# Another order of the first eight steps, and eight weight sums moved from VectorE to TensorE

## The chip, the cores and the metric

The kernel runs on one core of one Trainium2 chip. The metric is the device time of one execution in microseconds; the time before is the median of three runs. Engines are named as in the profile: PE is the matmul engine TensorE (PEld its weight loads), DVE is VectorE, ACT is ScalarE, POOL is GpSimd, and SP is the engine on whose queue nearly all transfers are issued.

## What is computed

Linear attention without softmax, a normalisation by head, and a dense layer pair with softplus between its matrices:

```python
kv  = einsum('bhsd,bhse->bhde', k, v)          # 8 batches, 8 heads, 576 rows, 64 wide
out = einsum('bhsd,bhde->bhse', q, kv)
rms = sqrt(mean(out * out, -1) + 1e-6)
x   = (out / rms * g_norm) as 4608 x 512       # float32
h   = x @ w_in                                 # 512 x 2048, given in 64-bit floats
g   = softplus(h)
return g @ w_out                               # 2048 x 512, given in 64-bit floats
```

## The kernel before

**Tiles and stages.** The 4608 rows of x are 36 tiles of 128; three tiles make a block of 384 rows, twelve blocks in all. The 2048 hidden columns are sixteen chunks of 128. In the first stage blocks 0 to 3 are taken through chunks 0 to 3 and blocks 4 to 11 through chunks 0 to 5. One pair of block and chunk is a *step* (function `step`, 64 steps). `mm1` (L843) makes the chunk's h for the block in one PSUM bank of the ring `h`, ACT applies softplus (L865) and takes the high part (L867), DVE makes the low and the third part (L854, L858), and `mm2` (L850) adds the product with w_out to three sum banks `s0` to `s2`, one for each tile. When the block's chunks are done, `leave` evicts each sum bank with ACT (L895) and stores it to DRAM as a partial sum (L910). Two further phases, with blocks of 512 rows and pairs of chunks, take the rest by a scheme with seven products for eight (L1030, L1100). In the last phase `enter` loads a tile's two partial sums and adds them into the bank with which that phase begins (L886, L889), and `leave` writes the output.

**Precision.** Every matmul operand is cut into a high, a low and a third part in the format fp32r, and three matmuls stand for one product. `split` does it for x (L620, L623, L626), `split_weight` for the weights.

**Weights.** `weight(j, ...)` handles one of the 32 pieces, j = 2c for w_in of chunk c and j = 2c + 1 for w_out. It loads the 64-bit words (L403, 512 KB), and DVE and ACT turn them into one float: `square` (L414), `high1`, `high2`, `mask`, `power`, `rest` (L418, L422, L427, L435, L440) give a large part `t` and a small part `p`, and `total` (L444) adds the two on DVE into a buffer `w` of the SBUF ring `m`. `split_weight` then reads `w`: ACT takes the high part (L481 for w_in, L483 for w_out), DVE the low part (L488, L491), ACT scales the low part (L494). For chunks 0 to 3 (`by_pe`) PE forms the rest in an `h` bank (L505, L506), and ACT writes the third part from there (L509). The ring `h` has two banks.

**x.** `kv_of` forms kv of a batch on PE from K and V loads (L676). `rows(t)` makes one tile of x: q turned (L756, L763), product with kv (L700), square (L773), reduce (L704), root on POOL (L707, L708), norm (L712), turned by PE (L718) and, for tiles 0 to 5, split straight from the bank. x is also stored to DRAM (L782, L783); from tile 6 on, `x_again` loads and splits it. The split x of a block lies in one of two `xv` buffers, which the block gives back with the mm1 of its last chunk.

**What sets the order.** `Plan` writes out the order of every engine's queue beforehand. Each task has an engine, a price in ns, the tasks that it comes after, the buffers that it takes and gives, and a position `pos`. The planner takes, among the tasks that could begin within 150 ns of the first, the one with the smallest `pos`. A task's end, as its successors see it, is start + price + a hand-over of its engine (`HANDOVER`, 120 to 250 ns; L181, L194). Positions come from the number of the step and from lists of constants `P0` to `P7`: when each weight is fetched (`FETCH`) and converted (`CONVERT`), when rows are made, and so on. Where PE would stand idle early on, the planner puts in a filler, `warm` (L1181), a matmul of the identity whose result nobody reads; it ends with step 6.

The steps are listed by `ORDER` (L363), block by block. Besides its x and weights, the mm1 of step s waits for the mm1 before it and for the finished w_out of step s - 2 (L861, L862).

Of the kernel before, what the change touches and what calls it, by code (L numbers as in the profile page):

```python
# [8 lines left out]
F32 = mybir.dt.float32  # L9
# [4 lines left out]
ALU = mybir.AluOpType  # L14
# [4 lines left out]
P = 128  # L19
# [36 lines left out]
class Plan:  # L56
# [19 lines left out]
    def slot(self, ring):  # L76
        return Slot(ring)
# [11 lines left out]
    def order(self):  # L89
# [5 lines left out]
        ready = {}  # L95
# [28 lines left out]
        while left:  # L124
            best = None
            for engine, tasks in ready.items():
                options = []
                for t in tasks:
                    at = max(engine_free[engine], t.ready)
                    if t.size:  # L130
                        at = max(at, dma_free - 2500)
                    for i, s in enumerate(t.take):
                        others = sum(u.ring == s.ring for u in t.take[:i])
                        if engine == "SP" and s.ring in ("m", "n"):
                            others += self.KEEP
                        if len(free[s.ring]) <= others:
                            break
                        at = max(at, sorted(free[s.ring])[sum(u.ring == s.ring for u in t.take[:i])][0])
                    else:
                        options.append((at, t))  # L140
                if not options:
                    continue
                first = min(at for at, _ in options)
                options = [(at, t) for at, t in options if at <= first + self.SOON]
                small = [o for o in options if engine == "PE" and o[1].kind != "all"]
                if small:
                    rest = [o for o in options if o[1].kind == "all"]
                    if kind != "all":
                        options = [o for o in small if o[1].kind == kind] or small
                    elif rest and len(small) < self.TOGETHER and (  # L150
                            min(o[1].pos for o in small) + self.PATIENCE > min(o[1].pos for o in rest)):
                        options = rest
                at, t = min(options, key=lambda o: (o[1].pos, o[0]))
                if engine == "PE" and self.spare and self.spare[-1].start is None:
                    ring, run, ns, _ = self.spare
                    begin = max(engine_free["PE"], self.BEGIN, min(free[ring])[0] if free[ring] else at)
                    if begin + ns <= at:
                        s = Slot(ring)
                        at, t = begin, Task("PE", ns, lambda s=s: run(s), [], None, [s], [s], 0)
                        t.kind = "all"  # L160
                        s.readers = 1
                if best is None or at < best[0]:
                    best = (at, t)
            if best is None:
                raise RuntimeError("the plan is stuck at " + str([(e, t.pos, [s.ring for s in t.take if not free[s.ring]]) for e, ts in ready.items() for t in ts][:20]))
            at, t = best
            if t in ready[t.engine]:
                ready[t.engine].remove(t)
                left -= 1
            for s in t.take:  # L170
                place = min(free[s.ring])
                free[s.ring].remove(place)
                s.place = place[1]
                if t.pos is not None:
                    coming[s.ring] = coming.get(s.ring, 0) - 1
            if t.engine == "PE":
                t.ns += self.SWITCH.get((kind, t.kind), 0)
                kind = t.kind
            t.start = at
            engine_free[t.engine] = at + t.ns  # L180
            t.end = at + t.ns + self.HANDOVER[t.engine]  # L181
            if t.size:
                dma_free = max(dma_free, at + t.ns) + t.size
                t.end = dma_free + (self.LANDING if dma_free > self.FILLED else 2000)
            for s in t.give:
                s.readers -= 1
                last_read[id(s)] = max(last_read.get(id(s), 0), t.end)
                if not s.readers:
                    free[s.ring].append((last_read[id(s)], s.place))
                    retire(s.ring)  # L190
            for u in users.get(id(t), ()):
                waiting[id(u)] -= 1
                if not waiting[id(u)]:
                    u.ready = max([a.end for a in u.after] + ([u.follows.start] if u.follows else []), default=0)  # L194
                    ready.setdefault(u.engine, []).append(u)
            done.append(t)
        return sorted(done, key=lambda t: t.start)
# [3 lines left out]
def kernel(  # L201
# [24 lines left out]
    nc = tc.nc  # L226
    B, H, S, D = q.shape
    d_model, d_ff = moe_w_in.shape
# [17 lines left out]
    STEPS = [(ph, n, p) for ph in (1, 2) for n in range(n_wide) for p in PAIRS[ph - 1][n]]  # L246
    LAST = 2

    P0 = [-45.94, -26.77, -11.8, 0.28, -29.91, -5.64, -2.86, 3.84, -103.4, -98.98, -69.3, -76.66, -68.5, -24.67, -23.22, -34.97, 8.15, -43.02, 7.47, 9.69, 7.18, 18.16, -12.1, 4.75, 1.0, 95.98, -6.45, 6.38, 7.69, 5.17]
    P4 = [-30.17, -6.08, 16.93, -33.9, -22.35, -28.91, -17.33, -7.12, -9.75, -2.59, 0.87, 2.93, -12.14, -3.26, 0.98, 3.76, 7.8, -3.0, -2.25, 7.68, 20.89, 50.27, -0.5, -0.13, 26.66, 22.67, -11.61, -5.55, 2.74, 0.64, -0.48, 1.34, 0.64, 1.68, -8.4, -1.37]  # L250
    P5 = [1.24, -5.69, -2.28, 1.58, 5.58, 0.43, 5.83, -7.56, 3.01, -2.95, 3.18, 1.42, -14.52, 0.57, -1.29, -1.34]
    P6 = [-0.39, 4.6, -0.28, -2.24, -0.01, 1.05, 1.77, -3.9, -2.15, 0.85, 1.85, -1.74, 6.34, -2.44, -0.13, 3.82, 7.89, 0.51]
    P7 = [-23.78, -17.98, -11.85, -14.93, 0.41, 1.61, 7.35, 2.7, -25.02, -6.6, -15.2, -4.48, -2.14, 0.64, 2.93, 0.97, 4.67, 5.36, 3.33, 6.57, -10.37, 2.36, -14.11, -9.89, -7.11, 12.91, -2.89, 14.55, 12.59, 9.35]
    CONVERT, FETCH, EARLY, LATER = P0[:8], P0[8:16], P0[16:27], P0[27:]
    P1 = [48.8, 48.65, 66.31, 74.64, 125.35, 131.27, -11.31, 54.26, 67.75, 469.13, 282.82, 195.86]
    P2 = [22.14, 35.93, 25.02, 37.31, 52.38, 81.67, 74.61, 116.65, 106.27, 111.35, 100.82, -152.23, 99.52, 221.41, 428.54, -173.95, 119.58, -155.43, 317.87, 212.07, -7.69]
    P3 = [3.0, 2.86, 5.84, -16.31, 1.53, 3.03, 3.55, -20.64, 3.15, 2.55, 1.38, 1.52, 1.27, 0.75, 2.42, -1.39]
    SPLIT = {p: (P1[i], P1[6 + i]) for i, p in enumerate((2, 3, 4, 5, 6, 7))}
    TAKEN = {c: (P2[c - 6], P2[4 + c]) for c in range(6, 16)}
    LEAD, APART, AHEAD, MM2, LATE, SPLIT_G = P3[0], P3[1], P3[2], P3[3:11], P3[11:14], P3[14]  # L260
# [99 lines left out]
        return src[e * NP:(e + 1) * NP].rearrange("p s d -> s p d")  # L360


    ORDER = [(n, c) for n, cs in CHUNKS.items() for c in cs]  # L363
    first_step = {}
    last_step = {}
    for s, (n, c) in enumerate(ORDER):
# [27 lines left out]
    def weight(j, pos, fetch_pos, behind):  # L394

        c, of_out = divmod(j, 2)
        raw, w = slot("rawb" if j % 2 and c < 8 else "raw"), slot("m")
        words = 2 if wide else 1

        def fetch():  # L400
# [6 lines left out]
        if wide:  # L407
# [41 lines left out]
            d2 = add("DVE", 690, high2, [d1], pos, [], [raw])  # L449
            d3 = add("DVE", 690, mask, [d2, a1], pos, [])  # L450
            over_done.append(add("ACT", 910, beyond, [d3], pos + (4 if c < 4 else 0), [], [sq]))
            d4 = add("DVE", 430, power, [d3], pos, [p, w])
            d5 = add("DVE", 690, rest, [d4], pos, [], [raw])
            ready = add("DVE", 690, total, [d3, d5], pos, [], [t, p])
        else:
            ready = add("DVE", 450, lambda: nc.vector.tensor_copy(new(w, [P, d_model]), raw.tile[:, :, 0]),
                        [f], pos, [w], [raw])
# [370 lines left out]

    def step(s):
        n, c = ORDER[s]  # L830
        cs = CHUNKS[n]
        h, g, gv = slot("h"), slot("g"), slot("gv")
        if c == cs[0]:
            sums[:] = [slot(f"s{i}") for i in range(TB)]
# [21 lines left out]
        def less():  # L856
# [3 lines left out]

        a = add("PE", 2100, mm1, x_split[n] + factors_done[0, c] + [m for _, m in mm1s[-1:]] +  # L861
                (factors_done[1, ORDER[s - 2][1]] if s > 1 else []), s, [h],  # L862
                ([xv] if c == cs[-1] else []) + ([w_in] if s == last_step[c] and c != 4 else []))
        mm1s.append((s, a))
        a = add("ACT", 490, lambda: nc.scalar.activation(new(g, [P, NT]), h.tile, func=AF.Softplus, scale=1.0 + E),  # L865
                [a], s, [g], [h])
# [14 lines left out]
    def enter(t, bank, pos):  # L881

        both_of = []
        for src, st in part[t]:
            pt = slot("m")
            both_of.append((pt, add("SP", 350, lambda pt=pt, src=src: nc.sync.dma_start(out=new(pt, [P, d_model]), in_=src),  # L886
                                    [st], pos - 2.5, [pt], [], 900, behind=pos - 3.5)))
        (p0, l0), (p1, l1) = both_of
        return add("DVE", 700, lambda: nc.vector.tensor_tensor(out=new(bank, [P, d_model]), in0=p0.tile, in1=p1.tile, op=ALU.add),  # L889
                   [l0, l1], pos, [bank], [p0, p1])  # L890

    def leave(ph, t, bank, done, pos):

# [4 lines left out]
        if ph == LAST and BY_PE <= t < n_tiles - TB:  # L898
# [7 lines left out]

            add("SP", 1600, store, [a], pos, [], [ot], 750)
            return
        dst = out[t * P:(t + 1) * P] if ph == LAST else dram.tile([P, d_model], F32, name=f"part{ph}_{t}")
        st = add("SP", 350, lambda: nc.sync.dma_start(out=dst, in_=ot.tile), [a], pos, [], [ot], 720)  # L910
        part.setdefault(t, []).append((dst, st))

# [304 lines left out]
```

## Time and profile before

| | us |
|---|---|
| median of three runs | 872.99 |
| lowest and highest run | 872.97, 874.07 |
| the profiled execution | 873.68 |
| its span, first to last instruction | 871.7 |
| DVE add of `t` and `p`, L444, median of 32 | 0.691 |
| eviction of a sum bank, L895, median of 72 | 0.598 |
| add of two partial sums, L889, median of 36 | 0.694 |
| mean granted clock of PE | 0.994 |

The span is measured on the engines; the time of an execution has some 2 us around it. A group of the profile gives the line of the kernel, the engine, what is written from what, the number of instructions, their busy time and the mean of one. A window gives the busy time of each engine between two times counted from the start of the span. A chain of waits is followed back from the last instruction. The matmul of a true fp32 product stands in the profile as two records.

### The profile page before, as it was taken

To read this page: it belongs to the slowest core of one execution; us is meant where nothing else is said; L and a number is where in the kernel's file an instruction comes from. 1 tells how busy PE (TensorE), PEld (TensorE's weight loads), DVE (VectorE), ACT (ScalarE), POOL (GpSimd) and SP (SyncE) were. 2 spreads that over 40 slices of the span, in tenths; PEclk is the share of its full clock that TensorE was granted. 3 is DMA by queue.
4 is the path that set the end of the run, shared out by engine and by line. 5 is a ranking of instruction groups with operands and counts; after the bars stand their busy time and mean duration, and the time that the engine had idled before them with its cause. 6 is when DMAs were issued, how large, how long until landed. Compare 5 with 4: busy or idle time off the path is not lost.

```text
span 871.7 us, 17016 instructions
## 1 busy us (share of the span) xinstructions
PE 858.2 (98%) x6464; PEld 761.2 (87%) x6464; DVE 703.9 (81%) x992; ACT 521.4 (60%) x979; POOL 78.3 (9%) x79
## 2 busy tenths in 40 slices
PE   7899999999999999999999999999999999999998
PEld 5678888989898899988998988888899899999996
DVE  7888898988788788798988789877788766878873
ACT  5776564445353567766657556654877555566653
POOL 0351234121112300000000000000000000000000
PEclk9899999999999999999999999999999999999999
DMA  9999999898993765427544546656364653777764
GB/s 270 275 231 206 283 243 253 152 267 210 221 175 102 178 194 170 156 85 243 183 156 147 182 157 192 196 158 180 110 195 136 237 162 107 243 225 234 236 189 129
DMA packets 239634, 167.07 MB, mean 192 GB/s; under 512 B 106304, under 2 KB 198464, under 8 KB 239552
## 3 DMA queue, kind: packets, MB, share of 16 engines
q1 hardware_dynamic: 239392, 165.99, 68.2%
q8 instruction: 50, 0.82, 0.4%
q14 instruction: 32, 0.26, 0.1%
q10 hardware_dynamic: 160, 0.00, 0.0%
HBM read 112.98 MB, written 52.95 MB: 190 GB/s over the span
## 4 chain that ended last, share of the span: by engine, by line
PE 94%; DMA 2%; DVE 2%; ACT 1%; POOL 1%; issue 0%; SPq 0%; POOLq 0%; DVEq 0%; ACTq 0%
PE banks L1100 30%; PE banks L1030 28%; PE banks L850 16%; PE banks L843 15%; PE banks L700 2%; PE banks L676 2%; DMA loads<-in_k_dram 1%; DMA loads<-in_v_dram 1%; PE banks L1181 1%; PE banks L718 0%; POOL r L708 0%; DVE half L712 0%; PE banks L756 0%; SPq L403 0%; DVE units L623 0%
## 5 line engine op out<-in xcount | busy, mean ns | idle before, releaser
L1100 PE MATMUL banks<-pieces,gv 128*128 128x512 f32 x696 | 217.9, 394 | 0.0
L843 PE MATMUL banks<-units,pieces 128*128 128x384 f32 x768 | 145.8, 338 | 0.0
L850 PE MATMUL banks<-pieces,gv 128*128 128x512 f32 x576 | 145.5, 396 | 0.0
L843 PEld LDWEIGHTS banks<-units,pieces 128*128 128x128 f32 x768 | 135.1, 188 | 5.1
L1100 PEld LDWEIGHTS banks<-pieces,gv 128*128 128x128 f32 x696 | 121.2, 189 | 18.1
L1100 PE MATMUL banks<-pieces,g_False 128*128 128x512 f32 x348 | 136.4, 392 | 0.1
L1030 PEld LDWEIGHTS banks<-units,pieces 128*128 128x128 f32 x948 | 126.9, 190 | 8.3 <-ACT banks L1075 1.3
L1030 PE MATMUL banks<-units,pieces 128*128 128x256 f32 x948 | 132.5, 282 | 0.0
L850 PEld LDWEIGHTS banks<-pieces,gv 128*128 128x128 f32 x576 | 106.3, 187 | 21.0
L865 ACT ACTIVATE half<-banks 128x384 f32<-128x384 f32 x64 | 31.4, 490 | 92.3 <-PE banks L843 92.2
L1090 DVE TENSOR_TENSOR gv<-g_True,gv 128x1024 fp32r<-128x1024 f32 x48 | 58.8, 1224 | 33.9 <-ACT gv L1087 33.9
L1100 PEld LDWEIGHTS banks<-pieces,g_False 128*128 128x128 f32 x348 | 65.4, 188 | 15.3 <-DVE g_False L1093 0.6
L1079 DVE TENSOR_TENSOR g_True<-banks,g_True 128x512 f32<-128x512 f32 x48 | 33.2, 691 | 38.8 <-PE banks L1030 34.6
L708 POOL TENSOR_TENSOR r<-r,half 128x8 f32<-128x8 f32 x36 | 63.7, 1770 | 3.0
L1057 ACT ACTIVATE g_True<-banks 128x256 f32<-128x256 f32 x96 | 36.8, 383 | 39.7 <-PE banks L1030 39.2
L1093 DVE SCALAR_TENSOR_TENSOR g_False<-gv 128x1024 fp32r<-128x1024 f32 x48 | 58.7, 1224 | 1.3
L993 DVE TENSOR_TENSOR units<-loads,units 128x1024 fp32r<-128x1024 f32 x42 | 51.2, 1219 | 8.7 <-ACT units L990 8.7
L1030 PEld LDWEIGHTS banks<-units,w 128*128 128x128 f32 x396 | 52.5, 189 | 2.8
L1030 PE MATMUL banks<-units,w 128*128 128x256 f32 x396 | 54.8, 281 | 0.0
L990 ACT ACTIVATE units<-loads 128x1024 fp32r<-128x1024 f32 x42 | 44.4, 1058 | 17.0 <-PE banks L1030 11.0
L996 DVE SCALAR_TENSOR_TENSOR units<-units 128x1024 fp32r<-128x1024 f32 x42 | 51.4, 1223 | 1.6
L1087 ACT ACTIVATE gv<-g_True 128x1024 fp32r<-128x1024 f32 x48 | 51.0, 1062 | 1.5
(116 smaller groups left out, 1301.8 us busy)
## 6 DMA issues: line engine op xcount, KB each, us to landing
loads<-x SPq DMA_DIRECT2D x180, 128.0 KB, 2.8
part<-m SPq DMA_DIRECT2D x72, 256.0 KB, 2.9
m<-part SPq DMA_DIRECT2D x72, 256.0 KB, 3.4
loads<-form SPq DMA_DIRECT2D x45, 256.0 KB, 3.6
form<-loads SPq DMA_DIRECT2D x36, 256.0 KB, 2.7
raw<-in_moe_w_in_dram SPq DMA_DIRECT2D x16, 512.0 KB, 4.7
loads<-in_k_dram SPq DMA_DIRECT2D x32, 256.0 KB, 4.7
loads<-in_v_dram SPq DMA_DIRECT2D x32, 256.0 KB, 4.9
```

What stands on the lines that cost most here:

```text
L708: nc.gpsimd.tensor_tensor(out=r.tile, in0=r.tile, in1=half, op=ALU.pow)
L843: nc.tensor.matmul(hp, lhsT=w_in.tile[:, i, kd * P:(kd + 1) * P], rhs=xv.tile[:, i, kd], start=(m == 0), stop=(m == 3 * KD - 1))
L850: nc.tensor.matmul(mine[i].tile, lhsT=gv.tile[:, m, i * P:(i + 1) * P], rhs=w_out.tile[:, m], start=(c == cs[0] and m == 0), stop=(c == cs ...
L990: nc.scalar.activation(part_of(0, F32R), xl.tile if m > 1 else xl.tile[:, 0], func=AF.Copy, scale=DOWN)
L993: nc.vector.tensor_tensor(out=part_of(1, F32R), in0=xl.tile if m > 1 else xl.tile[:, 0], in1=part_of(0), op=ALU.subtract)
L996: nc.vector.scalar_tensor_tensor(out=part_of(2, F32R), in0=part_of(1), scalar=-RADIX, in1=part_of(0), op0=ALU.mult, op1=ALU.add)
L1030: nc.tensor.matmul(place(q), lhsT=w[:, m, at:at + P], rhs=dst.tile[:, m, v, kd] if u < 6 else dst.tile[:, m, kd], start=(u == 0 and not m ...
L1057: nc.scalar.activation(dst, src, func=AF.Softplus, scale=1.0 + E)
L1087: nc.scalar.activation(gvt(0, F32R), gt(), func=AF.Copy, scale=DOWN)
L1090: nc.vector.tensor_tensor(out=gvt(1, F32R), in0=gt(), in1=gvt(0), op=ALU.subtract)
L1093: nc.vector.scalar_tensor_tensor(out=gt(F32R), in0=gvt(1), scalar=-RADIX, in1=gvt(0), op0=ALU.mult, op1=ALU.add)
L1100: nc.tensor.matmul(mine[i].tile, lhsT=(gvt(m, F32R) if m < 2 else gt(F32R))[:, c, i * P:(i + 1) * P], rhs=outs[c].tile[:, m], start=fresh ...
```

## The change

The steps of blocks 0 and 1 are put in another order: block 0 with chunks 0 and 1, block 1 with chunks 0 and 1, then block 0 with chunks 2 and 3, then block 1 with the same. Each of the four segments starts its sum banks anew and evicts them, so the six tiles of these blocks have two partial sums from the first stage, and `enter` adds three instead of two for them. x of a block is given back at the block's last step (`block_end`).

For chunks 0 to 3 the sum of `t` and `p` is no longer made by DVE into SBUF: PE multiplies both by the identity in true fp32 and adds them in an `h` bank, which `split_weight` then reads in place of the `m` buffer and gives back after the low part.

In the planner, a task whose predecessor runs on the same engine no longer counts that engine's hand-over. The constants `P0` to `P7` have new values throughout.

```diff
-                    u.ready = max([a.end for a in u.after] + ([u.follows.start] if u.follows else []), default=0)
+                    u.ready = max([a.end - (a.engine == u.engine) * self.HANDOVER[a.engine] for a in u.after] + ([u.follows.start] if u.follows else []), default=0)
...
-    P0 = [-45.94, -26.77, -11.8, 0.28, -29.91, -5.64, -2.86, 3.84, -103.4, -98.98, -69.3, -76.66, -68.5, -24.67, -23.22, -34.97, 8.15, -43.02, 7.47, 9.69, 7.18, 18.16, -12.1, 4.75, 1.0, 95.98, -6.45, 6.38, 7.69, 5.17]
+    P0 = [-128.72, 2.52, -23.28, -15.6, -15.23, -6.01, -95.85, 4.65, -201.64, -165.73, -72.05, -123.34, -43.94, -25.16, 39.57, 1.61, -1.73, -62.54, 38.93, 12.87, 5.0, 26.88, -5.04, 2.5, 0.2, 228.43, 18.38, 6.39, 12.98, 9.31]
...
-    ORDER = [(n, c) for n, cs in CHUNKS.items() for c in cs]
+    SEGMENTS = [(n, cs) for cs in ((0, 1), (2, 3)) for n in (0, 1)] + [(n, cs) for n, cs in CHUNKS.items() if n > 1]
+    ORDER = [(n, c) for n, cs in SEGMENTS for c in cs]
+    SEGMENT = [cs for _, cs in SEGMENTS for _ in cs]
+    block_end = {n: s for s, (n, _) in enumerate(ORDER)}
...
-        raw, w = slot("rawb" if j % 2 and c < 8 else "raw"), slot("m")
+        raw, w = slot("rawb" if j % 2 and c < 8 else "raw"), slot("h" if wide and c < 4 else "m")
...
-            d4 = add("DVE", 430, power, [d3], pos, [p, w])
+            d4 = add("DVE", 430, power, [d3], pos, [p, w] if c >= 4 else [p])
             d5 = add("DVE", 690, rest, [d4], pos, [], [raw])
-            ready = add("DVE", 690, total, [d3, d5], pos, [], [t, p])
+            if c < 4:
+                bank = w
+
+                def total_by_pe():
+                    y = new(bank, [P, d_model])
+                    nc.tensor.matmul(y, lhsT=ident, rhs=t.tile.bitcast(F32), start=True, stop=False)
+                    nc.tensor.matmul(y, lhsT=ident, rhs=p.tile.bitcast(F32), start=False, stop=True)
+
+                ready = add("PE", 1870, total_by_pe, [d3, d5], pos, [bank], [t, p])
+            else:
+                ready = add("DVE", 690, total, [d3, d5], pos, [], [t, p])
...
-        cs = CHUNKS[n]
+        cs = SEGMENT[s]
...
-                ([xv] if c == cs[-1] else []) + ([w_in] if s == last_step[c] and c != 4 else []))
+                ([xv] if s == block_end[n] else []) + ([w_in] if s == last_step[c] and c != 4 else []))
...
-        (p0, l0), (p1, l1) = both_of
-        return add("DVE", 700, lambda: nc.vector.tensor_tensor(out=new(bank, [P, d_model]), in0=p0.tile, in1=p1.tile, op=ALU.add),
-                   [l0, l1], pos, [bank], [p0, p1])
+        (p0, l0), (p1, l1), *rest = both_of
+        a = add("DVE", 700, lambda: nc.vector.tensor_tensor(out=new(bank, [P, d_model]), in0=p0.tile, in1=p1.tile, op=ALU.add),
+                [l0, l1], pos, [bank], [p0, p1])
+        for p, ld in rest:
+            a = add("DVE", 700, lambda p=p: nc.vector.tensor_tensor(out=bank.tile, in0=bank.tile, in1=p.tile, op=ALU.add),
+                    [a, ld], pos, [], [p])
+        return a
```

More of the change, by code (lines that the diff above doesn't have):

```diff
@@ L247 @@
     LAST = 2
-    P0 = [-45.94, -26.77, -11.8, 0.28, -29.91, -5.64, -2.86, 3.84, -103.4, -98.98, -69.3, -76.66, -68.5, -24.67, -23.22, -34.97, 8.15, -43.02, 7.47, 9.69, 7.18, 18.16, -12.1, 4.75, 1.0, 95.98, -6.45, 6.38, 7.69, 5.17]
-    P4 = [-30.17, -6.08, 16.93, -33.9, -22.35, -28.91, -17.33, -7.12, -9.75, -2.59, 0.87, 2.93, -12.14, -3.26, 0.98, 3.76, 7.8, -3.0, -2.25, 7.68, 20.89, 50.27, -0.5, -0.13, 26.66, 22.67, -11.61, -5.55, 2.74, 0.64, -0.48, 1.34, 0.64, 1.68, -8.4, -1.37]
-    P5 = [1.24, -5.69, -2.28, 1.58, 5.58, 0.43, 5.83, -7.56, 3.01, -2.95, 3.18, 1.42, -14.52, 0.57, -1.29, -1.34]
@@ L252 @@
-    P6 = [-0.39, 4.6, -0.28, -2.24, -0.01, 1.05, 1.77, -3.9, -2.15, 0.85, 1.85, -1.74, 6.34, -2.44, -0.13, 3.82, 7.89, 0.51]
-    P7 = [-23.78, -17.98, -11.85, -14.93, 0.41, 1.61, 7.35, 2.7, -25.02, -6.6, -15.2, -4.48, -2.14, 0.64, 2.93, 0.97, 4.67, 5.36, 3.33, 6.57, -10.37, 2.36, -14.11, -9.89, -7.11, 12.91, -2.89, 14.55, 12.59, 9.35]
+    P0 = [-128.72, 2.52, -23.28, -15.6, -15.23, -6.01, -95.85, 4.65, -201.64, -165.73, -72.05, -123.34, -43.94, -25.16, 39.57, 1.61, -1.73, -62.54, 38.93, 12.87, 5.0, 26.88, -5.04, 2.5, 0.2, 228.43, 18.38, 6.39, 12.98, 9.31]
@@ new lines @@
+    P4 = [-78.81, -20.05, -27.05, -7.09, 3.62, 19.83, -39.76, -12.2, -60.32, 3.77, 3.74, -10.19, -25.46, -21.21, 2.64, -10.23, 7.08, -13.5, 0.3, 22.18, 53.83, 83.24, -17.34, -10.33, 139.87, 66.56, -13.3, -8.91, -0.45, -2.62, -19.18, 8.87, -1.11, 59.51, -0.11, -28.64]
+    P5 = [0.34, -19.52, -6.44, 20.56, -2.51, 9.49, -3.72, -8.4, 24.33, 27.09, -12.91, -2.91, -23.65, 7.78, -9.5, -4.74]
+    P6 = [5.04, 3.06, 3.77, 13.36, 1.81, -4.04, 4.71, 0.73, 5.1, -40.34, 9.61, 11.57, 2.44, 7.48, 9.03, 0.67, 5.75, 4.12]
@@ L254 @@
+    P7 = [-21.13, -38.84, -28.2, -23.18, -13.73, 24.3, 3.44, 3.44, -40.91, -14.5, -25.21, -40.79, -25.76, -22.24, 8.94, 0.73, 27.33, -47.65, -21.94, -14.77, -10.72, -6.08, -19.08, -18.45, -21.76, -21.82, -8.3, -8.99, 48.78, 57.69]
     CONVERT, FETCH, EARLY, LATER = P0[:8], P0[8:16], P0[16:27], P0[27:]
-    P1 = [48.8, 48.65, 66.31, 74.64, 125.35, 131.27, -11.31, 54.26, 67.75, 469.13, 282.82, 195.86]
-    P2 = [22.14, 35.93, 25.02, 37.31, 52.38, 81.67, 74.61, 116.65, 106.27, 111.35, 100.82, -152.23, 99.52, 221.41, 428.54, -173.95, 119.58, -155.43, 317.87, 212.07, -7.69]
@@ L257 @@
-    P3 = [3.0, 2.86, 5.84, -16.31, 1.53, 3.03, 3.55, -20.64, 3.15, 2.55, 1.38, 1.52, 1.27, 0.75, 2.42, -1.39]
+    P1 = [51.73, 55.69, 57.28, 68.17, 122.26, 131.2, 29.4, 32.63, 69.99, 377.75, 163.75, 149.88]
+    P2 = [42.32, 28.39, 19.4, 42.46, 39.5, 80.96, 78.84, 112.89, 102.06, 100.98, 145.35, -354.27, 105.22, 320.34, 378.47, -556.15, 118.69, -366.77, 137.15, 125.41, -7.98]
+    P3 = [4.02, 1.66, 6.68, -30.72, 0.59, 4.16, 3.9, -24.08, 3.26, 3.35, 3.31, 2.49, -12.87, -13.65, 1.39, 0.9]
     SPLIT = {p: (P1[i], P1[6 + i]) for i, p in enumerate((2, 3, 4, 5, 6, 7))}
@@ L908, in leave @@
             return
-        dst = out[t * P:(t + 1) * P] if ph == LAST else dram.tile([P, d_model], F32, name=f"part{ph}_{t}")
+        dst = out[t * P:(t + 1) * P] if ph == LAST else dram.tile([P, d_model], F32, name=f"part{len(part.get(t, ()))}_{t}")
         st = add("SP", 350, lambda: nc.sync.dma_start(out=dst, in_=ot.tile), [a], pos, [], [ot], 720)
```

## The prediction

> **What bounds the kernel now.** I read the page from the top (busy time, then the slices), then the windows of the first 84 us, once for all engines and once for line 1181 alone, then PE's waits, and the groups of the operations that are touched.
>
> ```profile
> PE 858.2 (98%) x6464; PEld 761.2 (87%) x6464; DVE 703.9 (81%) x992; ACT 521.4 (60%) x979; POOL 78.3 (9%) x79
> ...
> PE   7899999999999999999999999999999999999998
> ```
> ```profile
> 8.50:20.00 11.50, 10.84 (x107) 7.74 (x108) 9.37 (x17) 7.80 (x15) 0.00 (x0) 0.85 1.20 295
> 20.00:35.00 15.00, 12.83 (x206) 9.97 (x201) 12.03 (x21) 10.40 (x23) 4.17 (x4) 0.77 1.06 281
> 35.00:47.00 12.00, 10.32 (x152) 7.56 (x149) 10.82 (x19) 9.89 (x20) 5.61 (x6) 1.00 1.07 241
> 47.00:84.00 37.00, 35.54 (x451) 29.70 (x450) 32.13 (x56) 24.23 (x49) 13.44 (x13) 1.00 0.99 220
> ```
> ```profile
> 8.50:20.00 11.50, 5.79 (x16) 3.08 (x16) 0.85 1.20 295
> 20.00:35.00 15.00, 3.97 (x8) 2.01 (x8) 0.77 1.06 281
> 35.00:47.00 12.00, 4.23 (x13) 2.21 (x13) 1.00 1.07 241
> 47.00:84.00 37.00, 0.99 (x3) 0.38 (x2) 1.00 0.99 220
> ```
> ```profile
> 84.00:872.00 788.00, 783.75 (x5553) 702.60 (x5551) 634.41 (x871) 465.60 (x871) 54.16 (x50) 1.00 0.65 186
> ```
>
> The columns of the windows: length, busy PE, PEld, DVE, ACT, POOL, clock, DMA share, GB/s; in the second table PE and PEld of line 1181 alone. PE is the bound from about 84 us to the end: the last window lacks 4.25 us, of which 0.27 us lies behind the span and nearly all the rest is the drain after the last matmul. Nothing after 84 us can be won except there. Before it, "busy" deceives: line 1181 is a filler that multiplies the identity into a spare bank and serves nobody. Fillers plus idle PE are 5.79 + 0.66 = 6.45 us up to 20 us, 3.97 + 2.17 = 6.14 up to 35, 4.23 + 1.68 = 5.91 up to 47, and 0.99 + 1.46 = 2.45 up to 84: **20.95 us of holes**, all that better ordering can win. (Ahead of 8.5 us PE waits for the first K and V loads; I leave that as it is.) In the same stretch DVE is 80 to 90% busy and the DMA share is about 1, so both feed PE only just.
>
> PE's waits between 8.5 and 84 us are each small; the only ones over 1 us in sum are these, in the list for the first 85 us (the second lies ahead of 8.5 us):
>
> ```profile
> PE banks L676 <- DMA loads<-in_v_dram: 3.2, 2, 1.9
> PE banks L1181 <- DVE ident_r L1141: 1.6, 1, 1.6
> ```
>
> The fillers stand where the written-out order has nothing ready. The first useful mm1 starts at 47.01 us (chain of waits). Its x was ready early enough: the third tile's `less` (L626) is done at 43.6. Block 1's last `less` ends at 55.3, yet its first mm1 runs at 73.96, because steps 1 to 3 want the weights of chunks 1, 2 and 3 first; mm1 0,1,2,3 of block 0 stand at 47, 52, 56 and 67 us.
>
> **What the Trainium skill says.** "Perfetto Trace Analysis" (opening note) calls matmul busy time a poor measure, since matmuls are pipelined; the table above agrees, 14.98 us of PE's 69.5 busy us are filler. "FP8 and Floating Point Precision" (TensorE Precision Notes): true fp32 takes four passes of the array. The trace agrees in form: the code issues 8 fp32 matmuls for each kv piece (L676) and the profile shows 16 records. "TensorE: Matmul & The Clock Gate" (§ What happens when you issue a matmul) says that matmuls stay in program order, only weight loads move ahead; so an added matmul that waits holds back all matmuls behind it. No line of this trace shows it by itself. "PSUM — Partial Sum Buffer" counts eight banks, one matmul output in at most one bank; so a weight sum in PSUM occupies one of the two `h` banks.
>
> **The change part by part.**
>
> *Weight sums on PE.* Removed: 8 adds on DVE (L444, group mean 687 ns), 5.5 us. Added: 16 fp32 matmuls of 128x512. Price: 9 one-pass 128x512 matmuls of L850 take 2.10 us in the chain, 0.233 each; four passes 0.93, two matmuls 1.87, eight weights **14.9 us**. Lower bound 4 x 512 columns at the speed of L843 (12 x 384 columns in 2.10 us, 0.456 ns a column), 0.93 again; upper bound from the kv piece: 16 records, two side by side, so 8 x 64 columns in 1.15 us, which makes 18.4 us for eight, but small matmuls carry more overhead. I take 14.9. At clock 0.77 to 0.85 four early ones cost 1 to 2 us more. The reads of the sum from PSUM cost nothing: DVE from banks (L623) 688 ns against 687 and 746 for L491 and L488; ACT from banks (L509) 604 against 634. The latency of a weight grows from 0.69 to 1.87 us plus a handover; hidden, since conversion of the next weight lies beside it, unless PE's queue has other work in front.
>
> *The order of steps.* Nothing added on PE: 8 steps with the same matmuls. The first four steps need four weights instead of eight. DVE's needs for them: per tile reduce, norm, low, less (0.68 + 0.69 + 0.69 + 0.69 = 2.75), six tiles 16.5 us; per weight 0.42 + 0.69 + 0.68 + 0.43 + 0.69 + 0.72 = 3.63 without the sum, four 14.5 us. That is 31 us of DVE at 0.84 busy (32.22 of 38.5 us up to 47), 37 us from about 5 us on: all four steps can be fed by about 42 us. By DMA: K and V of two batches 4.7 MB, q 1.6, four weights 2.1, six x stores 1.6 = 10 MB at the 281 GB/s of the second window, some 36 us. So block 0 is ready about 33 to 37 us, block 1 at 42 to 45, against 43.6 and 55.3. Four steps are 4 x 4.2 = 17 us of PE work, all before the weights of chunks 2 and 3 are needed.
>
> *What the new order asks for.* xv has two buffers. Block 0 holds its one until its last step, now the sixth, so x of block 2 can be split only after that mm1; until step 9 wants it lie 10.5 us of PE work against 3 x 1.38 = 4.1 us on DVE. Costs nothing, 3 us if DVE lags. Each of the two blocks leaves its sums twice: 6 evictions on ACT (L895, 0.59 us; 3.5 us beside 60% busy ACT), 6 stores and 6 loads of 256 KB on SP's queue (about 0.33 to 0.43 us to issue), and 6 more adds on DVE (L889, 0.69 us, 4.1 us) behind 645 us, where DVE is 69 to 88% busy (three windows of 20 us from 640 on: 16.03, 17.50 and 13.87 us). The next block's mm1 covers the eviction (2.1 us). Nothing, bound 1 us.
>
> *The planner's hand-over term and the new constants.* They change the orders of all queues and add no instruction. After 84 us PE has no idle time to lose, so a better order gains nothing there; a worse one can cost. I take 0, from -1 (the drain) to +3.
>
> *The sum.* Holes after the change: up to 35 us 12.6 us of holes face four sums (7.5 us at full clock, about 9 at the granted one); dependences leave some 6 unfilled. From 35 to 47 PE now has two to four steps in hand: 1 instead of 5.9. Up to 84: 2. Together 9, so 12 us are won and 14.9 are paid: **+3 us**. The profiled execution took 873.68 us, its span 871.7 and 2.0 around it; +3 makes 876.7, and the median of the runs lies 0.7 below the profiled one: **876.0**.
>
> **Rivals.**
>
> *A, the forecast:* the four late sums fall into saturated PE time and cost 7.5 us in full, the early four are mostly hidden, the earlier steps win about 5. 872.5 to 879.
>
> *B, faster:* up to 47 us PE does 38.5 - 18.5 = 20.0 us of useful work now; four or five sums (8 to 10 at the granted clock) and two and a half steps (10.5) make some 40 for 38.5 us, so PE could fill its holes down to 4 us. Then 17 are won, 14.9 paid: -2, so 871; with no hole left and the clock at 1.0 instead of 0.85 and 0.77 for useful work, -6. For: DVE is relieved exactly where it is 80 to 90% busy, and steps 0 to 3 wait for four weights only. Against: each added sum is a fresh place where PE's ordered queue waits for DVE. It decides as soon as the holes fall below 6 us.
>
> *C, the h banks:* each weight holds one of two banks from the sum to `low`: 1.9 + 0.7 + 0.7 and hand-overs, 4 us and more, eight times 32 us, while mm1 and the third parts (L505) want the same two. If half of the four late holds stops an mm1, 8 us of holes come on top of 2: holes 14 to 17, +8 to +11, 881 to 884. For: both users stand in the same 20 us. Against: one bank suffices for mm1 at 2.1 + 0.5 us in a step of 4.2.
>
> *D, the loads bind:* DMA share 1.07 up to 47 us and the landings of K and V (4.75, 6.29 and 6.51 us in the chain) set the start; the steps move forward only slightly, holes 12 to 14, +6 to +8: 880. For: the chain's first long pieces are those loads. Against: two to four weights, 0.5 MB each, can be postponed.
>
> **How the numbers follow.** A 0.45, B 0.30, C 0.13, D 0.12. What a measurement of this kernel can't tell from no change is 0.2%, 1.75 us (871.2 to 874.7). A lies within it with a third of its chance. Faster 0.27, same 0.19, slower 0.54. Range: B's middle to the edge of C, 869 to 881; A alone 872.5 to 879.
>
> **What would show it.** Right: line 444 keeps 24 of 32 adds; 16 new matmul records or 32, about 0.93 us for each matmul; first mm1 below 40 us, the third mm1 at about 45; fillers and idle after 8.5 us about 9 us; after 84 us PE busy throughout but for a similar drain. Wrong: holes of 15 or more (C if mm1 waits behind banks or DVE's low, D if behind loads), holes under 6 (B), a matmul far from 0.93 us, or idle PE in phase 2.

## The result and the profile after

| | before | changed |
|---|---|---|
| median, us | 872.98 (4 runs) | 878.70 (4 runs, 878.01 to 881.11) |
| ratio of the times | | 1.0068, 95% interval 1.0047 to 1.0089 |
| the profiled execution, us | 873.68 | 881.11 |
| its span, us | 871.7 | 878.9 |

The changed kernel is slower by 5.7 us, 0.7%. A later measurement of the same kernel gave the ratio 1.0064 (1.0043 to 1.0086). The profiled execution was the slowest of the four, so its span is 7.2 us longer.

First the windows of the first 84 us of the changed kernel, with the columns of the windows before: length, busy PE, PEld, DVE, ACT, POOL, clock, DMA share, GB/s.

```profile
8.50:20.00 11.50, 6.96 (x43) 4.30 (x44) 5.42 (x10) 3.38 (x7) 0.00 (x0) 0.56 1.00 246
20.00:35.00 15.00, 14.41 (x204) 9.62 (x205) 11.20 (x20) 11.19 (x24) 3.83 (x4) 1.00 0.97 240
35.00:47.00 12.00, 10.62 (x100) 9.08 (x99) 9.38 (x16) 8.83 (x18) 3.80 (x4) 0.86 1.06 291
47.00:84.00 37.00, 36.33 (x477) 27.69 (x476) 29.57 (x50) 26.15 (x53) 11.59 (x12) 1.00 1.07 236
```

The same windows for the filler alone, line 1198 in this kernel:

```profile
8.50:20.00 11.50, 1.90 (x2) 0.53 (x2) 0.56 1.00 246
20.00:35.00 15.00, 2.15 (x6) 0.98 (x6) 1.00 0.97 240
35.00:47.00 12.00, 0.73 (x2) 0.30 (x2) 0.86 1.06 291
47.00:84.00 37.00, 0.00 (x0) 0.00 (x0) 1.00 1.07 236
```

Holes, that is idle PE plus filler: 6.44 us up to 20, then 2.74, 2.11 and 0.67, together 11.96 us where the kernel before has 20.95. So 9.0 us of holes were won. The sums cost more than that. In the chain of waits of the changed kernel the two halves of a sum, and the first mm1s (L856), stand like this:

```profile
12.60 1.97 PE banks L689 x32
14.57 2.01 PE banks L462 x2
16.57 1.71 PE banks L463 x2
...
20.77 0.86 PE banks L462 x2
21.63 0.86 PE banks L463 x2
...
43.79 2.11 PE banks L856 x12
...
46.34 2.10 PE banks L856 x12
...
66.17 2.28 PE banks L856 x12
```

Two records are one fp32 matmul, 0.86 us at full clock; a sum takes 1.72 us, eight sums 13.7 us. The first sum took 3.72 us, since the clock was low after a long idle stretch. 13.7 - 9.0 is 4.7 us; with the 2.0 us of the slow first sum 6.7 of the 7.2 us of the profile are named.

Where the idle stretch comes from is told by PE's waits up to 90 us and by SP's queue (start, length, instruction), both of the changed kernel:

```profile
PE banks L689 <- DMA loads<-in_k_dram: 6.1, 1, 6.1
```
```profile
2.41 0.73 SPq L676 DMA_DIRECT2D g<-in_k_dram  x1
3.19 0.60 SPq L678 DMA_DIRECT2D loads<-in_v_dram  x1
3.84 0.46 SPq L406 DMA_DIRECT2D raw<-in_moe_w_in_dram  x1
4.35 0.51 SPq L678 DMA_DIRECT2D loads<-in_k_dram  x1
4.89 0.47 SPq L678 DMA_DIRECT2D loads<-in_v_dram  x1
5.41 0.47 SPq L678 DMA_DIRECT2D loads<-in_k_dram  x1
```

The first instruction of SP's queue is now a tail load, into a tile that DVE clears first (L1164, the first of two clearings ends at 2.38 us); it issues at 2.41 us, and the whole queue stands behind it. In the kernel before SP begins at 0.72 us with a weight, and the tail load is third:

```profile
0.72 0.43 SPq L403 DMA_DIRECT2D raw<-in_moe_w_in_dram  x1
1.22 0.49 SPq L665 DMA_DIRECT2D loads<-in_k_dram  x1
2.41 0.72 SPq L663 DMA_DIRECT2D g<-in_k_dram  x1
```

The first kv product starts at 12.60 us against 8.51 before. In a second profile of the changed kernel (e5 below), taken of an execution close to the median, it starts at 11.87 us behind a wait of 5.2 us, so a part of the 6.1 us belongs to the one execution.

### The profile page after: what moved, and what is told of

It reads as the page before. It is cut to its first block, busy times and chain, and to the rows that moved or that the text cites. A ratio compares the mean times of both kernels' runs of the same rounds, so it can differ in the third digit from the quotient of the medians.

```text
span 878.9 us, 17045 instructions
## 1 busy us (share of the span) xinstructions
PE 864.1 (98%) x6467; PEld 762.2 (87%) x6467; DVE 704.5 (80%) x990; ACT 523.8 (60%) x985; POOL 77.1 (9%) x79
## 4 chain that ended last, share of the span: by engine, by line
PE 95%; DMA 1%; SPq 1%; DVE 1%; ACT 1%; POOL 1%; issue 0%; POOLq 0%; ACTq 0%; DVEq 0%
PE banks L1117 30%; PE banks L1047 27%; PE banks L856 15%; PE banks L863 15%; PE banks L689 2%; PE banks L713 2%; DMA loads<-in_k_dram 1%; SPq L759 1%; PE banks L731 1%; PE banks L462 1%; DMA loads<-in_v_dram 1%; PE banks L463 0%; POOL r L721 0%; PE banks L769 0%; PE banks L518 0%
## 5 line engine op out<-in xcount | busy, mean ns | idle before, releaser
L856 PE MATMUL banks<-units,pieces 128*128 128x384 f32 x768 | 144.7, 338 | 0.0
L856 PEld LDWEIGHTS banks<-units,pieces 128*128 128x128 f32 x768 | 134.6, 188 | 4.4 <-issue 0.5
L721 POOL TENSOR_TENSOR r<-r,half 128x8 f32<-128x8 f32 x36 | 63.0, 1751 | 3.0
L1074 ACT ACTIVATE g_True<-g_True 128x512 f32<-128x512 f32 x48 | 30.3, 631 | 41.2 <-DVE g_True L1096 41.0
L1010 DVE TENSOR_TENSOR units<-loads,units 128x1024 fp32r<-128x1024 f32 x37 | 45.2, 1221 | 11.0 <-ACT units L1007 6.1
L1047 PEld LDWEIGHTS banks<-early,pieces 128*128 128x128 f32 x384 | 50.4, 190 | 2.3
L1047 PE MATMUL banks<-early,pieces 128*128 128x256 f32 x384 | 52.1, 282 | 0.0
L912 ACT ACTIVATE m<-banks 128x512 f32<-128x512 f32 x78 | 45.5, 596 | 10.8 <-PE banks L1117 7.3
```

The lines of the kernel that those rows point to most:

```text
L721: nc.gpsimd.tensor_tensor(out=r.tile, in0=r.tile, in1=half, op=ALU.pow)
L856: nc.tensor.matmul(hp, lhsT=w_in.tile[:, i, kd * P:(kd + 1) * P], rhs=xv.tile[:, i, kd], start=(m == 0), stop=(m == 3 * KD - 1))
L912: a = add("ACT", 690 if ph == LAST else 600, lambda: nc.scalar.activation(new(ot, [P, d_model]), bank.tile, func=AF.Copy, scale=scale if p ...
L1010: nc.vector.tensor_tensor(out=part_of(1, F32R), in0=xl.tile if m > 1 else xl.tile[:, 0], in1=part_of(0), op=ALU.subtract)
L1047: nc.tensor.matmul(place(q), lhsT=w[:, m, at:at + P], rhs=dst.tile[:, m, v, kd] if u < 6 else dst.tile[:, m, kd], start=(u == 0 and not m ...
L1074: nc.scalar.activation(dst, src, func=AF.Softplus, scale=1.0 + E)
```

## The experiments

Each was measured beside the kernel before on the same chip, which ran at a median of 874.5 to 874.7 us there; so the ratios are what to compare. e1 to e4, e5 to e8 and e9 to e12 ran on three different chips. "Clear half" stands for the edit of the third experiment.

| kernel | median, us | ratio to before, 95% interval | span of its profile |
|---|---|---|---|
| e5: changed, again | 880.05 | 1.0064 (1.0043 to 1.0086) | 877.9 |
| e1: all sums on DVE | 878.60 | 1.0045 (1.0030 to 1.0060) | 880.5 |
| e2: sums twice | 891.57 | 1.0196 (1.0175 to 1.0216) | 889.6 |
| e3: clear half | 877.47 | 1.0027 (1.0015 to 1.0040) | 875.3 |
| e4: 18 more fillers | 878.06 | 1.0041 (1.0025 to 1.0058) | 875.6 |
| e6: before, clear half | 876.04 | 1.0014 (1.0004 to 1.0024) | 873.9 |
| e7: clear half, all sums on DVE | 876.89 | 1.0028 (1.0016 to 1.0039) | 874.5 |
| e8: clear half, late sums on DVE | 876.06 | 1.0012 (1.0002 to 1.0021) | 873.2 |
| e9: clear half, early sums on DVE | 877.94 | 1.0032 (1.0018 to 1.0046) | 875.4 |
| e10: clear half, late sums twice | 883.32 | 1.0093 (1.0078 to 1.0109) | 881.0 |
| e11: clear half, no third partial sum | 877.08 | 1.0026 (1.0016 to 1.0036) | 876.4 |
| e12: e8 with 10 more fillers | 876.19 | 1.0010 (0.9999 to 1.0021) | 874.8 |

All edits leave the written-out orders of the changed kernel as they are; only what a task issues is altered. A part of the change cannot simply be taken back through the planner, because the constants belong to the whole; so the new order, the planner's term and the constants were tried only together.

**e1, the sums on VectorE at the same place.** All eight are moved back from PE to DVE.

```diff
-                    nc.tensor.matmul(y, lhsT=ident, rhs=t.tile.bitcast(F32), start=True, stop=False)
-                    nc.tensor.matmul(y, lhsT=ident, rhs=p.tile.bitcast(F32), start=False, stop=True)
+                    nc.vector.tensor_tensor(out=y, in0=t.tile.bitcast(F32), in1=p.tile.bitcast(F32), op=ALU.add)
```

> The changed kernel with each of the eight early sums written by one VectorE add into the same bank, at the same place of the written-out orders, instead of by two fp32 matmuls. Theory 1 (the matmuls of the sums lie on TensorE's path): 13.7 us of matmul go, and at most some of it turns into new idle time, so 5 to 12 us less than the changed kernel's 878.7, that is 867 to 873. Theory 2 (the late first loads and the cold clock behind them are the loss, the sums fill holes): 0 to 3 us less, 876 to 879. Theory 3 (the new order of steps and the new constants are the loss): the same or more, 878 to 882, since VectorE has 5.5 us more to do.

Measured 1.0045, some 2 us under the changed kernel, with overlapping intervals: theory 1 in its plain form falls. 13.7 us of matmul went and almost nothing came back. The windows of e1 show where the time went:

```profile
8.50:20.00 11.50, 7.01 (x48) 5.53 (x49) 8.37 (x14) 5.98 (x12) 0.00 (x0) 0.61 1.04 257
20.00:35.00 15.00, 10.46 (x182) 8.18 (x180) 9.75 (x18) 8.51 (x18) 4.37 (x4) 0.73 1.18 253
35.00:47.00 12.00, 11.56 (x87) 9.62 (x88) 8.75 (x15) 8.48 (x17) 3.80 (x4) 0.58 0.99 261
47.00:84.00 37.00, 33.47 (x473) 28.16 (x472) 31.87 (x56) 25.33 (x52) 10.39 (x10) 0.91 0.99 217
```

PE lies idle for 13.0 us of the 75.5 (7.2 in the changed kernel), and what it does runs at a clock of 0.58 to 0.73 for long. From 35 to 47 us it is busy 11.56 of 12 us and yet does only as much as 6.7 us at full clock would. The profiled execution was the slowest of the ten, with a mean clock of 0.981 over the whole span. The other nine had 0.984 to 0.988, the three executions of the changed kernel that were not profiled 0.996 to 0.997. So the lower clock belongs to this kernel, but the windows show it at its worst. That the added idle time lowers the clock fits; it was not tried apart.

**e2, the sums twice.**

```diff
+                    for _ in range(2):
                         nc.tensor.matmul(y, lhsT=ident, rhs=t.tile.bitcast(F32), start=True, stop=False)
                         nc.tensor.matmul(y, lhsT=ident, rhs=p.tile.bitcast(F32), start=False, stop=True)
```

> The changed kernel with the two matmuls of each early sum issued twice into the same bank (the second time over the first), everything else and all orders the same. Theory 1: the further 13.7 us lie on the path nearly in full, 10 to 14 us more, 889 to 893. Theory 2: holes are left for about half of it, 4 to 8 us more. Theory 3: under 4 us more.

Measured 1.0196, 0.013 above the changed kernel, 11 us of the 13.7 added, as theory 1 has it. From today's load upwards PE time is paid; from it downwards, as e1 shows, it isn't given back.

**e3, the first load no longer waits.**

```diff
     for x in tails:
-        nc.vector.memset(x, 0.0)
+        nc.vector.memset(x[64:], 0.0)
```

> The changed kernel with the clearing of the two tail tiles limited to the rows that no load writes (64 to 127), so that the first transfer on SP's queue, a tail load, doesn't wait for VectorE until 2.41 us. All orders the same. Theory 2: the whole queue of first loads comes 1.5 to 1.7 us earlier, TensorE starts earlier by as much and with less cold clock: 1.5 to 3 us less, 875.5 to 877. Theory 1: TensorE is short of work only there, so also some gain, 0.5 to 1.7 us. Theory 3: no change.

Measured 1.0027, about 3 us under the changed kernel, theory 2's size; the intervals don't overlap. SP's queue begins 1.69 us earlier, and in the chain of waits of e3 the first three mm1s stand 4.5 us earlier:

```profile
39.27 2.08 PE banks L856 x12
...
41.80 2.09 PE banks L856 x12
...
61.62 2.28 PE banks L856 x12
```

The clock from 8.5 to 20 us is 0.85 in place of 0.56. So 1.7 us on a queue became 4.5 us at the first step of this execution: the wait before the first kv product fell from 6.1 to 2.6 us, it starts 2.5 us earlier (10.10 us), and its 32 records take 1.15 in place of 1.97 us. Against the second profile of the changed kernel (e5), where the same mm1s stand at 41.27, 43.80 and 63.63 us, the gain is 2.0 us, close to what the queue gained.

**e4, more fillers ahead of the first product.** Before the planned order 18 filler matmuls were issued:

```diff
+    for _ in range(18):
+        nc.tensor.matmul(banks[:, 0].rearrange("r (a t) -> r a t", t=P), lhsT=ident_r, rhs=ident_r.unsqueeze(1).to_broadcast([P, 4, P]), start=True, stop=True)
```

> The changed kernel with 18 more filler matmuls of the identity at the very start of TensorE's queue, to bridge the 6.1 us without work before the first kv product, in which the granted clock fell to 0.56. Theory 2: the first sums and kv products run at full clock, 2 to 3 us less, about 876. Theory 1: under 1.5 us less, what the cold clock cost beyond the idle time. Theory 3: no change. If the loads arrive before the fillers end, up to 1 us more.

Measured 1.0041, about 2 us under the changed kernel, though the intervals overlap; the profile's clock is 1.00 in all four windows. That useless work seems to help fits theory 2. So the late loads as a loss are shown by e3; that the clock behind them adds to it is made likely by e4, not shown.

**e5, the changed kernel again**, unaltered.

> The changed kernel itself, unaltered, beside the kernel before on the same chip as the next three, so that they can be compared by ratio. All theories: a ratio of 1.004 to 1.009.

Its holes up to 84 us are 10.9 us by the same two tables, its span 877.9.

**e6, the clearing edit in the kernel before**, with the diff of e3.

> The kernel before with the clearing of the tail tiles limited to the rows that no load writes. There the tail load is the third on SP's queue and waited only 1.4 us in all (until 2.41 us), so theory 2 (the changed kernel suffers because its first load waits for the clearing) expects little here: 0 to 0.8 us less than before. If the whole gain of the same edit in the changed kernel were a general one, it would be 2 us or more here too.

Measured 1.0014: not faster, rather 1 us slower. So the gain of e3 is no general one; it belongs to a queue in which the tail load comes first. Why it costs here was not followed up.

**e7, e8, e9, the sums apart.** With the clearing edit, eight sums on DVE (e7), only the late ones, those of chunks 2 and 3 (e8), only the early ones, those of chunks 0 and 1 (e9). The edit of e8, beside that of e3:

```diff
+                    if c >= 2:
+                        nc.vector.tensor_tensor(out=y, in0=t.tile.bitcast(F32), in1=p.tile.bitcast(F32), op=ALU.add)
+                        return
```

> The changed kernel with both edits: the clearing limited to rows 64 to 127, and all eight early sums by one VectorE add at the same place of the orders. Theory 1 (the matmuls of the sums lie on the path): 5 us or more below the same kernel with the sums on TensorE (ratio 1.0027), so a ratio of 0.991 to 0.997. Theory 2 (holes of the new order are set by loads and VectorE, and the sums only fill them): within 2 us of it, ratio 1.0005 to 1.004.

> The same as the one before, but only the four sums of chunks 2 and 3 on VectorE; those of chunks 0 and 1 stay on TensorE. Theory 1 in the form of the prediction (late sums fall into saturated time and cost in full, early ones are mostly hidden): 4 to 7 us below the kernel with all sums on TensorE and the edited clearing (ratio 1.0027), a ratio of 0.995 to 0.998, and not slower than with all eight on VectorE. Theory 2: ratio 1.001 to 1.004.

> The changed kernel with the edited clearing, the four sums of chunks 0 and 1 by one VectorE add at the same place, those of chunks 2 and 3 on TensorE. With the three other combinations measured (both on TensorE 1.0027, both on VectorE 1.0028, only the late ones on VectorE 1.0012), the early sums should be better on TensorE by as much as the late ones are better on VectorE: ratio 1.003 to 1.006. If the early sums cost on TensorE too, the ratio falls below 1.002.

With the sums as they are the ratio is 1.0027 (e3), with all on DVE 1.0028: theory 2's range. Late ones on DVE give 1.0012, early ones 1.0032. The signs are those of the forecast (late sums cost, early ones don't), but the intervals of all three overlap with that of e3: the late ones are worth about 1.3 us, not 6.9, and the early ones nothing that can be told. The last window of e3 and of e8, and PE's waits in that of e8:

```profile
47.00:84.00 37.00, 36.23 (x432) 27.00 (x430) 27.73 (x48) 25.39 (x51) 14.24 (x14) 1.00 0.99 249
47.00:84.00 37.00, 32.87 (x428) 26.73 (x425) 31.15 (x55) 26.12 (x53) 14.16 (x14) 0.95 1.06 248
```
```profile
PE banks L521 <- DVE m L504: 2.3, 1, 2.3
PE banks L716 <- ACT half L789: 1.2, 1, 1.2
```

Now PE idles for 4.13 us there (0.77 in e3). It waits for the low part of a weight (L504) and for a square (L789), work of DVE and ACT. Of 6.9 us of matmul taken away 3.4 turned into waiting, and the clock fell to 0.95. DVE, however, now makes the sums as well; the longest wait ends directly behind one of them (L463):

```profile
49.84 0.70 DVE L463 TENSOR_TENSOR banks<-m,m 128x512 f32<-128x512 f32 x1
50.46 0.74 DVE L504 SCALAR_TENSOR_TENSOR m<-banks,g_col,pieces 128x512 f32<-128x512 f32 x1
```

How much PE would wait if the sums were on neither engine, no run tells.

**e10, the late sums twice**, the diff of e2 for chunks 2 and 3 only.

> The changed kernel with the edited clearing and the matmuls of the four late sums issued twice, 6.8 us more of matmul. If TensorE has no idle time left there (theory 1 from today's load upwards), 5.5 to 7 us more than with single sums, ratio 1.009 to 1.011. If loads and VectorE leave holes for it (theory 2), under 3 us more, ratio below 1.006.

Measured 1.0093, 5.8 us above e3 for 6.9 us of matmul. So the late sums do lie in saturated PE time, for whatever is added there. But the early ones seem to as well: doubling all eight cost some 11 us (e2), the late four 5.8 of it, which leaves about 5.5 us, uncertain by some 3, for the 6.9 us of the early four. (The two doublings started from different kernels, without and with the edit of e3.)

**e11, without the third partial sums.** The third load and add of six tiles are not issued.

```diff
-lambda pt=pt, src=src: nc.sync.dma_start(out=new(pt, [P, d_model]), in_=src),
+lambda pt=pt, src=src, left_out=len(both_of) > 1: None if left_out else nc.sync.dma_start(out=new(pt, [P, d_model]), in_=src),
...
-            a = add("DVE", 700, lambda p=p: nc.vector.tensor_tensor(out=bank.tile, in0=bank.tile, in1=p.tile, op=ALU.add),
+            a = add("DVE", 700, lambda: None,
```

> The changed kernel with the edited clearing, and without the load and the add of the third partial sum of tiles 0 to 5 in the last phase: six 256 KB loads and six VectorE adds of 0.69 us less, all orders the same; the output of these six tiles lacks the share of chunks 2 and 3. If the extra partial sums lie off TensorE's path (the prediction), the same time, ratio 1.0015 to 1.004. If they cost, 1 us or more less, below 1.0015.

Measured 1.0026 against 1.0027: the extra partial sums cost nothing in the last phase that these intervals, 0.1% to either side, can tell. Their evictions and stores in the first phase were left in, and not tried apart.

**e12, the best of it.**

> What the runs point to as the best of the changed kernel: edited clearing, late sums on VectorE, and ten more fillers at the start, which bridge the 2.6 us before the first kv product, so that the clock stays up. The clock of the first window was 0.85 there, so 0 to 1 us less than without the fillers (ratio 1.0012): 1.000 to 1.0015, no better than the kernel before. A ratio below 0.998 would mean that the cold start was worth more than the profiles show.

Measured 1.0010: the fillers add nothing to e8 that can be told, and no version was measured as faster than the kernel before.

## Why the prediction was right, and where it was off

The forecast was slower by 3 us, 876.0; measured is 878.7, inside its range and on its side. It lies nearer to rival D's 880 than to the forecast's own number, and of the steps behind that number some failed, so the closeness is in part luck:

- *Holes as the only thing to win, 20.95 us.* Right. After 84 us PE's idle time is 4.0 us in both profiles (783.75 of 787.7 us before, 790.89 of 794.9 after), all but a little of it the drain. Before 84 us busy time misled because 14.98 us of it were filler, not because matmuls are pipelined.
- *The sums, 14.9 us.* Measured 13.7 at full clock; close. One fp32 matmul took 0.86 us, 3.7 times the 0.233 us from which the price was made; the forecast took four times. (The two records of a matmul don't show the passes; this ratio speaks for nearly four.) The upper bound of 18.4 us came from a misread line: 1.15 us is the time of 32 records of L676, two kv pieces, not of 16. Nothing else was built on it.
- *Extra partial sums: nothing.* The last phase's share agrees with e11.
- *Block 0 ready at 33 to 37 us, block 1 at 42 to 45.* This is the step that failed. The last `less` of block 0 ends at 43.8 us, where the kernel before has 43.6; that of block 1 at 64.9, ten us later than the 55.3 before. The first mm1 ran at 43.79, the third, block 1's first, at 66.17. Even with the first loads early (e3) they run at 39.27 and 61.62. The estimate put the bytes of six tiles at the speed of one window, as if only these came and SP's queue never stood. But the queue began 1.7 us late, and six q loads (L759) took it from 7.31 to 14.81 us to issue; then the last pieces of K of batch 1, without which tiles 4 and 5 of block 1 can't be made, were issued only at 40.23 us. From the kv product behind them to the third mm1 another 16 us pass, through ACT, DVE and the roots on POOL (L721). Bytes and DVE time, which the forecast added up, hold neither of these waits. The first 50 us moved 11.75 MB against 13.14 before. Rival D's mechanism, loads that bind, is thus part of the answer, beside the forecast's own. It cost less than it might have: from 47 to 84 us PE found other work and was idle for 0.67 us only.
- *Holes afterwards, 9 us.* Measured 12.0 (10.9 in the second profile), 9.6 in e3; 12 to 14 was rival D's number. The term was mis-sized by the start, where 3.2 us more than forecast are left up to 35 us: 4 us more wait ahead of the first product, and the forecast left the stretch around 8.5 us "as it is", though the order of the first loads is set by the changed constants.
- *Clock.* The forecast named 1 to 2 us for four early sums at 0.77 to 0.85, and paid 14.9 us without them. One sum alone lost 2.0 us, in a window whose clock was 0.56 (1.1 us in the second profile).
- *Early sums hidden, late ones paid.* Not shown. As an added load the late ones are paid (e10), and the early ones, by the difference of e2 and e10, about as much. Taken away, they give back 1.3 us at most (e7 to e9); in e8, as in e1, PE then waits longer for DVE and ACT and its clock is lower. The forecast had no such asymmetry.
- *Rival C, the h banks.* PE's waits show no sign: its longest are for loads, ACT's q copies and DVE's parts of x.

Of block 1's late x, a line of SP's queue, three of the chain of waits and the last `less`, all of the changed kernel:

```profile
40.23 0.88 SPq L678 DMA_DIRECT2D loads<-in_k_dram  x2
```
```profile
48.43 1.55 PE banks L689 x48
...
53.71 1.85 POOL r L721
...
55.97 1.67 POOL r L721
```
```profile
64.24 0.69 DVE L639 SCALAR_TENSOR_TENSOR units<-units 128x512 fp32r<-128x512 f32 x1
```

Of the 5.7 us the late start is about 3, shown by e3 and, as the same edit gains nothing in the kernel before, by e6. For the rest the account of e3 closes, but it is an account and not a cause: PE's busy time without fillers is 14.2 us longer than before (the sums and the slow first one, against a lower clock in the kernel before), 11.4 us of holes are gone, and behind 84 us PE is idle for 0.8 us more, most of it a longer drain; together 3.6 us of span.

What stays open: with early loads and late sums on DVE the new order still isn't faster (e8, 1.0012). The new order of steps was not tried with constants made for it alone, so whether the order or the constants keep block 1 late can't be said.

## What to carry to other kernels

Moving work from a second engine to the bounding one pays only if the holes that are really closed are larger than the work, here 9.0 us against 13.7, though 20.95 were there. Count idle time and filler in the windows, and charge the work at its price there. Look at the first instruction of the transfer queue: if it waits for a buffer to be cleared, the whole start stands behind it. Doubling a piece of work and removing it can tell different things, as e2 and e1 do here, so do both.

## What the runs showed of the hardware that was not expected

PE's clock counted beside its work. After 6.1 us without work and a slow kv product, an fp32 matmul of 128x512 took 2.01 us in place of 0.86 (two records each). In e3 it took 2.01 us as well, after a wait of 2.6 us and a kv product that still ran at full speed (1.15 us). In the profile of e1, where PE lay idle more often, the clock stayed at 0.58 to 0.73 for nearly 40 us, and 13.7 us of work less bought about 2 us in the median. With 18 more matmuls that nobody reads, ahead of the first product, the windows show 1.00 (e4). The Trainium skill ("TensorE: Matmul & The Clock Gate", § Part 1) says that an idle window of about 3.4 us halves the clock. The matmul behind the 6.1 us agrees; that of e3 was as slow behind a shorter wait, so here the length of one wait alone doesn't tell.
